# The first attention's scores for two tiles at a time, its last blocks of x in another order

## The chip, the cores and the metric

The kernel runs on one core of one Trainium2 chip. The metric is the device time of one execution in microseconds (us). Five engines work side by side, each through its own instructions in order: TensorE (PE, with its weight loads PEld), VectorE (DVE), ScalarE (ACT), GpSimd (POOL) and SyncE (SP), which here only issues DMAs. TensorE writes its results into PSUM, from where DVE and ACT read them.

## The reference, cut to what matters

Four batches of attention with 8 heads, 768 rows and 64 columns a head, a local window of 96 and 8 global columns; its output, as x with 512 columns, goes through a mixture of four experts of two matrix products each.

```python
scores = scale * np.matmul(q, k.transpose(0, 1, 3, 2)) + bias   # bias: -slope * distance
scores = np.where(keep, scores, -1e9)                           # local window or global column
a = np.exp(scores - scores.max(-1)); a = a / (a.sum(-1) + 1e-9)
x = np.matmul(a, v)                                             # as (3072, 512)
for e in range(4):
    h = np.maximum(x @ w1[e], 0.0)
    out += p[:, e:e + 1] * (h @ w2[e])
```

## The kernel before, in words

**Two stages that overlap.** Attention works on one batch, on four pairs of heads, on six tiles of 128 rows. The expert layers of a batch work on 16 units, each a quarter of an expert's hidden columns: `first(i)` makes h of unit i with seven products of 128x384 (a scheme that makes eight block products of four quarter blocks out of seven), `second(i)` multiplies h with w2 and adds into the output. Each product is six matmuls, since every operand is held as a high part and a rest. Attention of batch b+1 is spread between the products of batch b. Only the attention of batch 0 has nothing beside it: it is the **start** (lines 821 to 832), with pools of its own, and is meant in all that follows.

**The start's flow.** `attention` (line 482) yields once a tile, n = 0 to 23, and four times more to drain (n = 24 to 27). `flow` (line 488) is a software pipeline of four tiles: at step n it issues the scores of tile n, the biased maximum (DVE) and exponentials (ACT) of tile n-1, the normalisation (DVE) of tile n-2, the transposes of tile n-3 (`turn`: PE, then an ACT copy), and every third step `weigh`, the product with v for three tiles, copied by ACT into x. `scores` (line 382) writes the two heads of a tile into two tiles ps0 and ps1 of two buffers each. `AHEAD` (line 211) says after which tile the next quarter of the next pair's q and k is transposed and copied. The pairs come in the order 0, 2, 1, 3, so x[:, 3], the last to be ready, gets its first half at n = 24 and its second at n = 27.

**Blocks of x.** The seven products of `first` do not take x but sums of its quarters: B11, B21, B22 and T1 to T4, made by `blocks` (line 597): ACT copies the high part, DVE or POOL subtracts it to get the rest, and DVE forms the sums in place in x. `blocks(0, (0,), po)` makes the half that pairs 0 and 2 give, from n = 17 on; `blocks(0, (1,))` the half of pairs 1 and 3, after the loop (line 845).

**Weights.** `load_w1` and `load_w2` are generators. Each loads a raw tile by DMA, waits `lead` steps, and makes copies (ACT) and rests (POOL) of it; for w1, POOL also forms four sums first, then `hold` steps pass. `work_chores` (line 814) advances every chore in hand by one step at each yield. For batch 0 a finished w1s or w2s tile is also stored into DRAM (`keep`) for the other batches.

**Order.** While `Ordered.on` is set, each engine runs in program order: through the start and through `first(0)`. It is unset when `done` reaches `ONSTEPS` (line 868), the number of yields of `first(0)`; after that the planner may move instructions. At that point the loads of batch 1's q, k and v are issued too (`next(att)`).

**Products.** `product` (line 723) takes one of four PSUM buffers pm in turn, so a product cannot begin before the readers of the fourth before it are done. `relu` (line 748) lets ACT write h's high part and puts the rest into the list `late`; DVE does it at the next `add`, and it reads pm too.

Of the kernel before, what the change touches and what calls it, by code (L numbers as in the profile page):

```python
# [9 lines left out]
F32 = mybir.dt.float32  # L10
# [15 lines left out]
def f32(ap):  # L26
    return ap.bitcast(F32)
# [158 lines left out]
def attn_moe_kernel(ctx: ExitStack, tc, q, k, v, n_global, n_local, domain_probs, w1, w2, out):  # L186
# [21 lines left out]

    PAIRS = (0, 2, 1, 3)

    AHEAD = ((0, 1, 1, 1, 1, 1), (1, 1, 1, 1, 1, 0), (1, 1, 1, 1, 0, 0), (0,) * NQT)

    BIASES = ((0, 1), (0, 3), (1, 0), (1, 2))

    ONSTEPS = 7

    PL = P + NGLOB
    fast = main.enter_context(tc.tile_pool(name="fast", bufs=1))
# [160 lines left out]
        po.tensor_copy(vg[NPREV:], vt[:NGLOB, :, 0:1, :].to_broadcast([NGLOB, 2, NQT, D]))  # L379
        return vg  # L380

    def scores(A, t, got, early):


        if early:
            ps = [A.ps.tile([P, 512], F32, name=f"ps{j}") for j in range(2)]
        else:
            both = A.ps.tile([P, 2, 2 * P], F32, name="ps")
            ps = [both[:, j] for j in range(2)]
        c0 = max(t - 1, 0) * PL + (0 if t == 0 else NGLOB)  # L390
        n = P if t == 0 else 2 * P
        for j in range(2):
            if early:
                own = slice(j * D, (j + 1) * D)
                win = got["k"].rearrange("p t c -> p (t c)")[own, c0 : c0 + n]
                te.matmul(ps[j][:, :n], got["q"][own, t, :], win, start=True, stop=True)
                continue
            win = got["k"][:, j].rearrange("p t c -> p (t c)")[:, c0 : c0 + 2 * P]
            for part in range(2):
                te.matmul(  # L400
                    ps[j][:, : 2 * P],
                    got[("q", t // TPH)][:, j, part, t % TPH * P : (t % TPH + 1) * P],
                    win,
                    start=(part == 0),
                    stop=(part == 1),
                )
        return ps

    def softmax(A, new, old):

# [71 lines left out]
    def attention(b, A, early=False):  # L482


        x = xs[b] = xp.tile([P, NPAIR, S], F32, name="x")
        tiles, turned = [None] * 4, []

        def flow(new=None):

            one, two, three, four = tiles  # L490
            if new:
                new["ps"] = scores(A, new["t"], gots[new["pr"]], early)
            if four:
                turned.append(four)
            ready = len(turned) == TPH
            if ready and not early:
                weigh(A, turned, x)
            if three and not early:
                turn(A, three)
            softmax(A, one, two)  # L500
            if three and early:
                turn(A, three)
            if ready and early:
                weigh(A, turned, x)
            if ready:
                turned.clear()
            tiles[:] = [new, one, two, three]

        def start(pr):

            nats[pr] = {n: next(load(A, src, b, pr, n)) for n, src in (("q", q), ("k", k), ("v", v))}

        def prepare(nat, got):

            got["v"] = nat
            prepare_q(A, nat["q"], 0, got)
            yield 1
            prepare_k(A, nat["k"], 0, got)
            yield 1
            prepare_q(A, nat["q"], 1, got)  # L520
            yield 1
            prepare_k(A, nat["k"], 1, got)
            yield 1
            nat["vg"] = windows(A, nat["v"])
            yield 1
            yield 1

        def prepare_all(pr):
# [12 lines left out]
            yield 1  # L541

        nats, gots = {}, [{} for _ in range(NPAIR)]
        if early:
            halves = [load(A, src, b, 0, n, 2) for n, src in (("q", q), ("k", k))]
            bias = biases(start_stack.enter_context(tc.tile_pool(name="setup", bufs=1)))
            next(bias)
            nats[0] = dict(zip(("q", "k"), (next(h) for h in halves)))
            for h in halves:
                next(h)  # L550
            nats[0]["v"] = next(load(A, v, b, 0, "v"))
            todo = [prepare_all(pr) for pr in PAIRS]
            next(bias)
            next(todo[0])
            start(PAIRS[1])
        else:
            start(0)
            yield
        for m, pr in enumerate(PAIRS):
            cur = gots[pr]  # L560
            if not early:
                prep = prepare(nats[pr], cur)
                for _ in range(3):
                    next(prep)
                    flow()
                    yield
            for t in range(NQT):
                if early:
                    if t == 2 and m + 2 < NPAIR:
                        start(PAIRS[m + 2])  # L570
                elif t in (1, 2, 3):
                    next(prep)
                    flow()
                    yield
                if t == NQT - 1 and not early and m + 1 < NPAIR:
                    start(PAIRS[m + 1])
# [20 lines left out]
    def blocks(b, ks=(0, 1), low=ve):  # L597
# [38 lines left out]
        rest(low, "T4", b11)  # L636
        yield 1


    NPR = FF // (2 * P)  # L640
    units = [(b, e, g) for b in range(B) for e in range(E) for g in range(NPR)]
# [59 lines left out]
    def load_w2(i, lead=7):  # L701

        if i >= len(units):
            return
        b, e, g = units[i]
        if b > 0:
            wts[(i, 2)] = fetch("w2s", (e, g, 2), [P, 2, 2, DM], lambda t: t)
            return
        raw = rp.tile([P, 2, DM], F32, name="raw2")
        sy.dma_start(raw, w2[e, g * 2 * P : (g + 1) * 2 * P, :].rearrange("(a p) m -> p a m", p=P))  # L710
        for _ in range(lead):
            yield 1
        dst = wp.tile([P, 2, 2, DM], F32R, name="w2s")
        wts[(i, 2)] = dst
        for f in range(2):
            ac.copy(dst[:, 0, f], raw[:, f])
            po.tensor_tensor(dst[:, 1, f], raw[:, f], f32(dst[:, 0, f]), op=ALU.subtract)
            yield 1
        waiting[(i, 2)] = (e, g, 2), dst

    hs = {}

    def product(i, a, x):

        pm = ps_mm.tile([P, 512], F32, name="pm")
        m = 0
        for kt in range(2):
            for wi, xi in ((0, 0), (1, 0), (0, 1)):
                te.matmul(
                    pm[:, :HALF], wts[(i, 1)][a][:, wi, kt, :], xb[x][:, xi, kt, :], start=(m == 0), stop=(m == 5)  # L730
                )
                m += 1
        return pm
# [3 lines left out]
    def work_late():  # L737

        while late:
            lo, src, hi = late.pop()  # L740
            ve.scalar_tensor_tensor(lo, src, 0.0, f32(hi), op0=ALU.max, op1=ALU.subtract)

    def first(i):

# [14 lines left out]
            add(pm[:, :HALF], pm, other)  # L759
            return pm[:, :HALF]  # L760

        p1, u, vv = (up.tile([P, HALF], F32, name=n) for n in ("p1", "u", "vv"))
        keep(i, 1)
        pm = product(i, "A11", "B11")
        ac.copy(p1, pm[:, :HALF])
# [51 lines left out]
                chores.remove(c)  # L817

    bp = main.enter_context(tc.tile_pool(name="bp", bufs=1))
    Ordered.on = True  # L820
    with ExitStack() as start_stack:
        A = Pools(start_stack, "start", st=1, kd=2, qd=2, nat=2, natv=3, pb=4, ps=2, pt=3, px=1, early=True)
        for n, _ in enumerate(attention(0, A, early=True)):
            if n == 9:
                chores += [load_w1(0, lead=2), load_w2(0, lead=3)]
            if n == 18:
                chores.append(load_w1(1, lead=2, hold=3))
            if n == 2 * NQT + 5:
                chores.append(blocks(0, (0,), po))
            work_chores()  # L830
        mix = mixture()
        next(mix)
    Ordered.on = False
    hp = main.enter_context(tc.tile_pool(name="hp", bufs=2))
    up = main.enter_context(tc.tile_pool(name="up", bufs=1))
    op = main.enter_context(tc.tile_pool(name="op", bufs=1))
    ps_mm = main.enter_context(tc.tile_pool(name="ps_mm", bufs=4, space=PSUM))
    A = Pools(main, "att", st=1, kd=1, qd=1, nat=1, natv=1, pb=2, ps=2, pt=2, px=0, early=False)
# [3 lines left out]
    per = E * NPR  # L842
    count, span = NPAIR * (6 + NQT) + 5, (13 * per - 12) * 0.97
    Ordered.on = True
    chores.append(blocks(0, (1,)))
    for _ in range(2):
        work_chores()
    for b in range(B):
        att = attention(b + 1, A) if b + 1 < B else iter(())
        emitted = done = 0  # L850
# [67 lines left out]
```

## Time and profile before

| what | value |
|---|---|
| runs | 1203.73, 1201.08, 1203.69 us; median 1203.69 |
| the profiled execution, time | 1202.66 us |
| the profiled execution, span of the core | 1200.9 us |
| ACT busy over the span | 494.7 us (41%) |
| DVE busy over the span | 824.1 us (69%) |
| mean granted TensorE clock | 0.993 |

The span runs from the first instruction to the last. The profile also has an answer by stretches (busy time of every engine between two points of the span, with the granted clock of TensorE: 0.50 is half speed) and a timeline, whose rows are: start, duration, engine, line, operation, output<-inputs, shapes, count, and in brackets how long the engine had been idle before and what released it. All helpers' instructions carry line 42, so rows are told apart by the names of their tiles. "pt" are transposes, "ps" scores, "px" the products with v, "pm" the products of the expert layers, "xB" and "xT" the blocks of x, "raw" a weight tile as loaded.

### The profile page before, as it was taken

Reading aid. Unit: us, or ns where it says so; the run is one execution under the profiler, and the core shown is the slowest. Engines: PE = TensorE matmul, PEld = TensorE weight load, DVE = VectorE, ACT = ScalarE, POOL = GpSimd, SP = SyncE. Lnnn points to the kernel's source line nnn. Section 1 sums busy time; section 2 is a strip of 40 time slices with the busy share of each in tenths; the row PEclk is TensorE's granted clock in tenths of the full one; section 3 lists DMA queues with packets and bytes.
Section 4 is the critical chain, followed back from the end, with each engine's and each line's share of the span. In section 5 each row is a group of like instructions: output and inputs, shape, how many; then the busy total and the mean of one; then the engine's idle time right before and its main releaser. Section 6 shows DMA issues by size and latency. Waiting matters only on the chain.

```text
span 1200.9 us, 18119 instructions
## 1 busy us (share of the span) xinstructions
PE 1174.0 (98%) x6624; PEld 1045.0 (87%) x6624; DVE 824.1 (69%) x1858; ACT 494.7 (41%) x1268; POOL 210.7 (18%) x222
## 2 busy tenths in 40 slices
PE   7889999999999999999999999999999999999997
PEld 5677889989889989989888989989898999999996
DVE  7776567667678767676668767676666766666665
ACT  6865655565643444444342434444443211111110
POOL 4645655645440000000002000000000000000000
PEclk9899999999999999999999999999999999999999
DMA  7456777787878567565746757574663655544532
GB/s 169 119 198 214 259 288 245 288 292 234 325 253 265 191 198 239 187 220 176 240 169 205 248 186 228 196 231 163 219 206 132 245 194 193 187 178 181 190 132 90
DMA packets 122704, 251.39 MB, mean 209 GB/s; under 512 B 83184, under 2 KB 91376, under 8 KB 106224
## 3 DMA queue, kind: packets, MB, share of 16 engines
q1 hardware_dynamic: 118864, 243.87, 61.1%
q10 hardware_dynamic: 3744, 6.30, 1.4%
q8 instruction: 54, 0.88, 0.3%
q14 instruction: 42, 0.34, 0.1%
HBM read 174.11 MB, written 52.43 MB: 189 GB/s over the span
## 4 chain that ended last, share of the span: by engine, by line
PE 88%; DMA 3%; ACT 2%; issue 2%; POOL 2%; DVE 1%; SPq 1%; POOLq 0%; ACTq 0%; DVEq 0%
PE pm L42 77%; PE pt L42 7%; PE ps L42 4%; DMA raw<-in_moe_w_dram 2%; POOL sums L42 1%; PE px L42 1%; POOL w2s L42 1%; ACT pb L42 1%; SPq L42 1%; DMA qd<-st_q 1%; DMA q<-in_q_dram 0%; ACT xT L42 0%; DVE x L42 0%; ACT xB L42 0%; ACT h L42 0%
## 5 line engine op out<-in xcount | busy, mean ns | idle before, releaser
L42 PE MATMUL pm<-w2s,h 128*128 128x512 f32 x2304 | 551.7, 393 | 4.5 <-DVE h L42 4.5
L42 PEld LDWEIGHTS pm<-w2s,h 128*128 128x128 f32 x2304 | 426.1, 188 | 92.5 <-DVE h L42 6.3
L42 DVE SCALAR_TENSOR_TENSOR acc<-pm,prob,acc 128x512 f32<-128x512 f32 x360 | 268.2, 749 | 148.8 <-PE pm L42 146.5
L42 PE MATMUL pm<-xT,w1s 128*128 128x384 f32 x1536 | 296.7, 338 | 0.2 <-ACT xT L42 0.2
L42 PEld LDWEIGHTS pm<-xT,w1s 128*128 128x128 f32 x1536 | 267.8, 189 | 2.5 <-issue 1.4
L42 PE MATMUL pm<-xB,w1s 128*128 128x384 f32 x1152 | 226.8, 338 | 1.8 <-DVE xB L42 1.5
L42 PEld LDWEIGHTS pm<-xB,w1s 128*128 128x128 f32 x1152 | 201.3, 188 | 7.0 <-DVE xB L42 1.8
L42 ACT ACTIVATE h<-pm 128x384 fp32r<-128x384 f32 x256 | 124.8, 491 | 177.7 <-DVE pm L42 174.3
L42 DVE SCALAR_TENSOR_TENSOR h<-pm,h 128x384 fp32r<-128x384 f32 x256 | 140.9, 552 | 13.1 <-ACT h L42 9.5
L42 ACT ACTIVATE pb<-pb,nmax 128x256 f32<-128x256 f32 (+1 forms) x192 | 93.1, 487 | 95.3 <-DVE nmax L42 94.6
L42 ACT COPY p<-pm 128x384 f32<-128x384 f32 x64 | 30.7, 479 | 191.1 <-PE pm L42 182.0
L42 POOL COPY vg<-v 32x768 f32<-32x768 f32 x16 | 13.2, 828 | 498.6 <-DMA v<-in_v_dram 435.9
L42 DVE TENSOR_TENSOR u<-pm,p 128x384 f32<-128x384 f32 x64 | 35.6, 556 | 73.4 <-PE pm L42 53.5
L42 DVE CUSTOM_DVE_ANT_0 pb<-ps,nbias 128x256 f32<-128x256 f32 (+1 forms) x192 | 71.7, 397 | 10.5 <-PE ps L42 5.7
L42 ACT COPY pT<-pt 128x512 f32<-128x512 f32 (+1 forms) x96 | 52.6, 548 | 58.1 <-PE pt L42 57.8
L42 DVE TENSOR_TENSOR pm<-pm,vv 128x384 f32<-128x384 f32 x128 | 71.7, 560 | 1.6 <-PE pm L42 1.4
L42 ACT ACTIVATE pb<-pb,zsum 128x256 f32<-128x256 f32 (+1 forms) x144 | 63.3, 485 | 18.0 <-DVE zsum L42 18.0
L42 PE MATMUL pt<-ident,pb 128*128 128x128 f32 x352 | 58.3, 283 | 2.7 <-DVE pb L42 1.5
L42 PEld LDWEIGHTS pt<-ident,pb 128*128 128x128 f32 x352 | 42.2, 143 | 15.4 <-ACT pb L42 3.6
L42 DVE TENSOR_TENSOR vv<-pm,u 128x384 f32<-128x384 f32 x64 | 35.7, 557 | 27.1 <-PE pm L42 26.2
L42 DVE TENSOR_TENSOR u<-pm,u 128x384 f32<-128x384 f32 x64 | 35.7, 557 | 25.1 <-PE pm L42 24.4
L42 POOL TENSOR_TENSOR w2s<-raw,w2s 128x512 fp32r<-128x512 f32 x32 | 41.0, 1296 | 57.6 <-ACT w2s L42 57.6
(88 smaller groups left out, 887.3 us busy)
## 6 DMA issues: line engine op xcount, KB each, us to landing
w1s<-kept SPq DMA_DIRECT2D x48, 1792.0 KB, 7.4
w2s<-kept SPq DMA_DIRECT2D x48, 1024.0 KB, 4.9
kept<-w1s SPq DMA_DIRECT2D x16, 1792.0 KB, 9.5
qd<-st_q SPq DMA_DIRECT2D x96, 192.0 KB, 4.7
raw<-in_moe_w_dram SPq DMA_DIRECT2D x32, 512.0 KB, 5.6
kept<-w2s SPq DMA_DIRECT2D x16, 1024.0 KB, 6.7
v<-in_v_dram SPq DMA_DIRECT2D x16, 384.0 KB, 3.4
out_dram<-acc ACTq DMA_DIRECT2D x24, 256.0 KB, 3.9
```

The lines of the kernel that those rows point to most:

```text
L42: ins = fn(*args, **kwargs)
```

## The change

Scores of the first attention are made for two tiles at once: `scores_early` puts the two heads' scores of tiles t and t+1 into two halves of one ps tile each, at every even tile; at odd tiles nothing is issued. For that the second halves of the first pair's k and q come one step earlier (`AHEAD`). `blocks(0, (1,))` gives way to `last_blocks`, in six steps: B11 at n = 19, B21 at n = 26, B22 and T2 after the loop, then one step each for T1, T3 and T4 at the yields of `first(0)`. The first product, A11 with B11, moves into the drain of the attention (`opening`, n = 25), with a ps0 tile for a pm, and brings the store of the first w1s tile with it; the other six come in another order, and that of S4 with B22 keeps its buffer until vv is there. w2's first tile is made at n = 14 and 15 (`lead=5`) and not at 12 and 13; w1's second tile starts one step earlier, ahead of `blocks` in the list, with a `hold` of 2 for 3. `ONSTEPS` is 6, as `first(0)` now yields six times.

```diff
-    AHEAD = ((0, 1, 1, 1, 1, 1), (1, 1, 1, 1, 1, 0), (1, 1, 1, 1, 0, 0), (0,) * NQT)
+    AHEAD = ((1, 1, 0, 1, 1, 1), (1, 1, 1, 1, 1, 0), (1, 1, 1, 1, 0, 0), (0,) * NQT)
...
-    ONSTEPS = 7
+    ONSTEPS = 6
...
+    def scores_early(A, t0, got):
+        heads = [A.ps.tile([P, 2, 2 * P], F32, name=f"ps{j}") for j in range(2)]
+        for t in (t0, t0 + 1):
+            c0 = max(t - 1, 0) * PL + (0 if t == 0 else NGLOB)
+            n = P if t == 0 else 2 * P
+            for j in range(2):
+                own = slice(j * D, (j + 1) * D)
+                win = got["k"].rearrange("p t c -> p (t c)")[own, c0 : c0 + n]
+                te.matmul(heads[j][:, t - t0, :n], got["q"][own, t, :], win, start=True, stop=True)
+        return [[heads[j][:, i] for j in range(2)] for i in range(2)]
...
+                elif new["t"] % 2 == 0:
+                    new["ps"], ahead[0] = scores_early(A, new["t"], gots[new["pr"]])
+                else:
+                    new["ps"] = ahead[0]
...
+    def last_blocks():
+        b11, b12, b21, b22 = (
+            xs[0][:, k : k + 1, s] for k in (1, 3) for s in (slice(0, HALF), slice(HALF, S))
+        )
...
+        high("B11", b11)
+        rest(po, "B11", b11)
+        yield 1
+        high("B21", b21)
+        rest(ve, "B21", b21)
+        yield 1
+        high("B22", b22)
+        ve.tensor_sub(b12, b22, b12)
+        ve.tensor_add(b11, b12, b11)
+        rest(ve, "B22", b22)
+        high("T2", b11)
+        rest(ve, "T2", b11)
+        yield 1
+        ve.tensor_sub(b22, b22, b11)
+        high("T1", b22)
+        rest(ve, "T1", b22)
+        yield 1
+        high("T3", b12)
+        rest(po, "T3", b12)
+        yield 1
+        ve.tensor_sub(b11, b21, b11)
+        high("T4", b11)
+        rest(ve, "T4", b11)
+        yield 1
...
+    def opening(A):
+        ups.append(sums_of_products())
+        keep(0, 1)
+        pm = product(0, "A11", "B11", A.ps.tile([P, 512], F32, name="ps0"))
+        ac.copy(ups[0][0], pm[:, :HALF])
...
+        if i == 0:
+            p1, u, vv = ups.pop()
+            relu(0, 0, last(product(i, "A12", "B21"), p1))
+            yield
+            pm4 = product(i, "S4", "B22")
+            yield
+            add(u, product(i, "S2", "T2"), p1)
+            yield
+            add(vv, product(i, "S1", "T1"), u)
+            relu(0, 1, last(pm4, vv))
+            yield
+            pm = product(i, "S3", "T3")
+            add(u, pm, u)
+            relu(1, 1, last(pm, vv))
+            yield
+            relu(1, 0, last(product(i, "A22", "T4"), u))
+            yield
+            return
...
             if n == 9:
-                chores += [load_w1(0, lead=2), load_w2(0, lead=3)]
-            if n == 18:
-                chores.append(load_w1(1, lead=2, hold=3))
+                chores += [load_w1(0, lead=2), load_w2(0, lead=5)]
             if n == 2 * NQT + 5:
-                chores.append(blocks(0, (0,), po))
+                chores += [load_w1(1, lead=2, hold=2), blocks(0, (0,), po)]
             work_chores()
+            if n == 3 * NQT + 1:
+                last = last_blocks()
+                next(last)
+            if n == 4 * NQT + 1:
+                opening(A)
+            if n == 4 * NQT + 2:
+                next(last)
...
-    chores.append(blocks(0, (1,)))
-    for _ in range(2):
-        work_chores()
+    chores.append(last)
+    work_chores()
```

More of the change, by code (lines that the diff above doesn't have):

```diff
@@ L380, in windows, with scores @@
         return vg
[L382 to L389, printed above, removed]
+    def scores(A, t, got):
+        both = A.ps.tile([P, 2, 2 * P], F32, name="ps")
         c0 = max(t - 1, 0) * PL + (0 if t == 0 else NGLOB)
-        n = P if t == 0 else 2 * P
         for j in range(2):
[L393 to L397, printed above, removed]
             win = got["k"][:, j].rearrange("p t c -> p (t c)")[:, c0 : c0 + 2 * P]
@@ L400, in scores @@
                 te.matmul(
-                    ps[j][:, : 2 * P],
+                    both[:, j],
                     got[("q", t // TPH)][:, j, part, t % TPH * P : (t % TPH + 1) * P],
@@ L406, in scores @@
                 )
-        return ps
+        return [both[:, j] for j in range(2)]
+    def scores_early(A, t0, got):
[8 more added lines that the diff above has]
+        return [[heads[j][:, i] for j in range(2)] for i in range(2)]
     def softmax(A, new, old):
@@ L485, in attention @@
         x = xs[b] = xp.tile([P, NPAIR, S], F32, name="x")
-        tiles, turned = [None] * 4, []
+        tiles, turned, ahead = [None] * 4, [], [None]
         def flow(new=None):
@@ L491, in flow @@
             if new:
-                new["ps"] = scores(A, new["t"], gots[new["pr"]], early)
+                if not early:
+                    new["ps"] = scores(A, new["t"], gots[new["pr"]])
+                elif new["t"] % 2 == 0:
+                    new["ps"], ahead[0] = scores_early(A, new["t"], gots[new["pr"]])
+                else:
+                    new["ps"] = ahead[0]
             if four:
@@ L637, in blocks, with high, rest @@
         yield 1
+    def last_blocks():
+        b11, b12, b21, b22 = (
+            xs[0][:, k : k + 1, s] for k in (1, 3) for s in (slice(0, HALF), slice(HALF, S))
+        )
+        def high(name, src):
+            ac.copy(xb[name][:, 0, 1:2], src)
+        def rest(eng, name, src):
+            eng.tensor_tensor(xb[name][:, 1, 1:2], src, f32(xb[name][:, 0, 1:2]), op=ALU.subtract)
+        high("B11", b11)
[22 more added lines that the diff above has]
+        yield 1
     NPR = FF // (2 * P)
@@ L721, in attn_moe_kernel, with product @@
     hs = {}
-    def product(i, a, x):
-        pm = ps_mm.tile([P, 512], F32, name="pm")
+    def product(i, a, x, pm=None):
+        if pm is None:
+            pm = ps_mm.tile([P, 512], F32, name="pm")
         m = 0
@@ L741, in work_late, with sums_of_products @@
             ve.scalar_tensor_tensor(lo, src, 0.0, f32(hi), op0=ALU.max, op1=ALU.subtract)
+    ups = []
+    def sums_of_products():
+        return [up.tile([P, HALF], F32, name=n) for n in ("p1", "u", "vv")]
+    def opening(A):
[3 more added lines that the diff above has]
+        ac.copy(ups[0][0], pm[:, :HALF])
     def first(i):
@@ L760, in last @@
             return pm[:, :HALF]
-        p1, u, vv = (up.tile([P, HALF], F32, name=n) for n in ("p1", "u", "vv"))
+        if i == 0:
[16 more added lines that the diff above has]
+            return
+        p1, u, vv = sums_of_products()
         keep(i, 1)
@@ L819, in attn_moe_kernel @@
     bp = main.enter_context(tc.tile_pool(name="bp", bufs=1))
+    up = main.enter_context(tc.tile_pool(name="up", bufs=1))
     Ordered.on = True
@@ L834, in attn_moe_kernel @@
     hp = main.enter_context(tc.tile_pool(name="hp", bufs=2))
-    up = main.enter_context(tc.tile_pool(name="up", bufs=1))
     op = main.enter_context(tc.tile_pool(name="op", bufs=1))
```

## The prediction, made before the changed kernel was run

> **What bounds the kernel now.** I read the page first: the shares and the chain that ended last.
>
> ```profile
> PE 1174.0 (98%) x6624; PEld 1045.0 (87%) x6624; DVE 824.1 (69%) x1858; ACT 494.7 (41%) x1268; POOL 210.7 (18%) x222
> ...
> PE 88%; DMA 3%; ACT 2%; issue 2%; POOL 2%; DVE 1%; SPq 1%; POOLq 0%; ACTq 0%; DVEq 0%
> ```
>
> TensorE sets the time nearly everywhere, and the change takes no matmul away. What it can win lies where PE waits or runs slowly: the start, up to about 81 us. Elsewhere it can win nothing; it can only move what the planner does after `first(0)`. So I read the start by stretches, cut where the granted clock (third number from the end) changes.
>
> ```profile
> core 0: us, PE busy (x) PEld busy (x) DVE busy (x) ACT busy (x) POOL busy (x), PEclk, DMA share, GB/s
> 22.00:35.00 13.00, 13.00 (x119) 8.86 (x116) 11.37 (x72) 12.48 (x40) 3.71 (x5) 1.00 0.69 186
> 36.40:39.80 3.40, 1.45 (x11) 1.00 (x11) 1.20 (x10) 2.67 (x9) 3.32 (x5) 0.98 0.01 3
> 39.80:43.00 3.20, 3.20 (x24) 2.23 (x24) 1.87 (x13) 3.20 (x12) 3.10 (x4) 0.50 0.01 3
> 49.90:53.30 3.40, 2.34 (x13) 1.17 (x10) 2.53 (x15) 2.57 (x11) 2.18 (x3) 1.00 0.38 18
> 53.30:60.10 6.80, 6.80 (x39) 4.75 (x38) 6.68 (x37) 4.73 (x16) 5.45 (x7) 0.50 0.01 4
> 63.50:66.90 3.40, 2.48 (x28) 1.88 (x28) 2.54 (x16) 3.40 (x11) 1.64 (x2) 1.00 0.01 2
> 70.40:73.90 3.50, 1.94 (x8) 1.33 (x9) 2.89 (x5) 0.89 (x2) 0.92 (x1) 0.99 0.94 393
> 73.90:77.20 3.30, 3.30 (x12) 3.10 (x11) 2.34 (x5) 1.34 (x3) 1.97 (x2) 0.50 1.02 417
> ```
>
> In 22 to 35 PE and ACT are both full (13.00 and 12.48 of 13.0). Then come three holes in PE (1.45 of 3.4, 2.34 of 3.4, 1.94 of 3.5), and behind each the clock is 0.50, for 3.2, 6.8 and 3.3 us. A stretch with 2.48 of 3.4 stayed at 1.00. So here a window of 3.4 us that is a third empty costs half speed in the next.
>
> **The change, part by part. w2 later.**
>
> ```profile
> 36.01 0.73 POOL L42 TENSOR_TENSOR sums<-raw 128x256 f32<-128x256 f32 x1 [6.91 <-DMA raw<-in_moe_w_dram]
> ...
> 37.13 0.62 ACT L42 CAST w2s<-raw 128x512 fp32r<-128x512 f32 x1 [2.24 <-DMA raw<-in_moe_w_dram]
> ...
> 43.55 0.82 POOL L42 COPY vg<-v 32x768 f32<-32x768 f32 x1 [0.65 <-POOL w2s L42]
> ...
> 47.20 1.28 POOL L42 TENSOR_TENSOR w1s<-sums,w1s 128x512 fp32r<-128x512 f32 x1 [0.70 <-ACT w1s L42]
> 49.50 1.97 POOL L42 TENSOR_TENSOR xB<-x,xB 128x384 fp32r<-128x384 f32 x2 [1.01 <-ACT xB L42]
> ...
> 51.49 0.56 DVE L42 TENSOR_TENSOR x<-x 128x384 f32<-128x384 f32 x1 [0.83 <-POOL xB L42]
> ```
>
> ACT, in order, stands 2.24 us at n = 12 for the raw w2, with the exponentials of the next tile behind it; hence the hole at 36.4. Two steps later the tile is long there, and w1's raw tile, which the copy at n = 13 needs, was there at 36.01. The two copies themselves only move. **What is late next is POOL**: it starts with w1's landing, and its rests must be done before those of the blocks at 49.50, which DVE awaits. From 36.01 to 48.48 POOL stood idle 0.65 and 0.70 us, both behind ACT; without these it ends at 47.13, the blocks' two rests at 49.1, and DVE's sum starts 2.4 us earlier than at 51.49. So the gain is ACT's, **-2.25**; it is 1.0 if POOL keeps its gaps (49.50 would then move by its wait of 1.01 alone).
>
> **Scores for two tiles.** The work of PE, DVE and ACT is the same. Saved is one change between scores and transposes per pair.
>
> ```profile
> 7.39 1.66 PE L42 MATMUL ps<-early_k,early_q 64*128 64x128 f32 x8 [0.57 <-ACT early_k L42]
> 8.97 0.90 PE L42 MATMUL pt<-ident,k 128*128 128x128 f32 x3
> ...
> 15.01 1.23 PE L42 MATMUL ps<-early_k,early_q 64*128 64x256 f32 x4
> 16.17 1.11 PE L42 MATMUL pt<-ident,pb 128*128 128x128 f32 x4
> ...
> 59.56 0.48 ACT L42 COPY x<-px 128x384 f32<-128x384 f32 x1 [1.79 <-PE px L42]
> ```
>
> One tile alone takes 16.17 - 15.01 = 1.16 us before the clock is up, the narrow first and the second tile together 1.58. I put the saving at 0.2 to 0.3 us for a pair, some 2 us of PE in all, but ACT, 96% busy in 22 to 35, lets only 0.5 of 13 through. Against it: in the first steps k's second half now stands ahead of the first exponentials on ACT, and a pair of scores (2.3 us at half speed) ahead of `turn`, for which ACT then waits. I count the first 20 us at 0 (from -1.0 to +0.7) and the rest at **-0.3**. PE's waits for a free ps buffer go as well, but the hole at 49.9 has DVE and POOL behind it: in n = 17 to 20 PE has no transposes of q and k left, so I let the half-speed stretch of 53 to 60 stand; if it goes, ACT's wait of 1.79 goes too.
>
> **Weights and blocks ahead of the end.** w1's second tile is copied at n = 21 to 24 and not 23 to 26, so two more copies stand ahead of the last exponentials, on an ACT that is full there (3.40 of 3.40 in 63.5 to 66.9).
>
> ```profile
> 66.03 0.42 ACT L42 CAST w1s<-raw 128x256 fp32r<-128x256 f32 x1
> ...
> 66.82 0.64 ACT L42 CAST w1s<-sums 128x512 fp32r<-128x512 f32 x1
> ...
> 68.73 0.48 ACT L42 COPY x<-px 128x384 f32<-128x384 f32 x1 [0.28 <-PE px L42]
> ```
>
> That is 0.42 + 0.64: **+1.0**. B11's copy at n = 19 (some 0.5, like the copy of x) falls ahead of ACT's wait of 1.79 and is hidden there; without that wait it costs its 0.5. The copies of p1 and of B21 take the places in the drain that two of the weights' copies leave: 0. POOL gets B11's rest on top, in a stretch where it is not the last. `opening`'s six matmuls fall into PE's empty 0.9 of the stretch 63.5 to 66.9: 0, at most +0.2.
>
> **The end: blocks and products.** All instants from here on are counted from the last copy into x, 68.73.
>
> ```profile
> 68.62 0.79 PE L42 MATMUL pm<-xB,w1s 128*128 128x384 f32 x3
> ...
> 79.55 1.30 PE L42 MATMUL pm<-xT,w1s 128*128 128x384 f32 x6
> 80.69 1.21 PE L42 MATMUL pm<-xB,w1s 128*128 128x384 f32 x6
> ...
> 69.25 1.22 DVE L42 TENSOR_TENSOR x<-x 128x384 f32<-128x384 f32 x1 [2.62 <-ACT x L42]
> ...
> 73.38 0.55 DVE L42 TENSOR_TENSOR x<-x 128x384 f32<-128x384 f32 x1
> ...
> 74.52 0.55 DVE L42 TENSOR_TENSOR xT<-x,xT 128x384 fp32r<-128x384 f32 x1
> ...
> 85.05 0.56 DVE L42 TENSOR_TENSOR u<-pm,u 128x384 f32<-128x384 f32 x1
> ...
> 88.65 0.55 DVE L42 SCALAR_TENSOR_TENSOR h<-pm,h 128x384 fp32r<-128x384 f32 x1
> ```
>
> Before, the last product begins at 79.55, or 10.8, and ends at 12.0. After, PE has its matmuls early: A12 with B21 needs nothing new. But there are four buffers pm, and the sixth product, A22 with T4, takes that of S4 with B22, which is held until vv is added, ACT has made h of it and DVE the rest, and that rest is emitted only behind the sum of the **fifth** product. In DVE's order these are 15 instructions: four for B12, B11, B22 and T2, the sum of A12, two for T1, u and a rest of h, two for T4, vv, the sum of S4, u, the rest of h. Eight such in a row take (88.65 - 85.05) / 7 = 0.51 each. So 15 take 7.7; T1 and T4 each wait for ACT between the sum and the rest (74.52 - 73.38 = 1.14, against 0.51, twice 0.63); DVE begins at 0.5 (69.25), and T2's wait and POOL's rest of T3 beside it (an instruction beside POOL took 1.22 at 69.25) add 0.3. The sixth product begins at 9.7 and, with 80.69 - 79.55 = 1.1, ends at 10.8: **-1.2**. PE has done the fifth at about 7.0 (it waits for the ninth DVE instruction, 5.9, for its own buffer) and stands still from 7.0 to 9.7. A window of 3.4 us that is four fifths empty is emptier than any of the three that were followed by clock 0.50; the dense products behind it then run at half speed for at least 3.3 us, which costs half of that, and part of a second window by where it falls: 1.65 to 3.4, I take **+1.9**. What the end of `blocks` before lost by its own stretch at 0.50 (73.90 to 77.20) is within its 12.0.
>
> Sum: -2.25 - 0.3 + 1.0 - 1.2 + 1.9 = **-0.85**. On the profiled execution's 1202.66 us (span 1200.9 and 1.8 around it) this gives **1201.8**. That execution is 1.0 below the median of the runs, 1203.69, and between their ends, so I do not correct for it.
>
> **The rivals. Gate open.** The wait at the end doesn't reach half speed, by the windows' phase or because DVE is quicker: 1201.8 - 1.9 = 1199.9; if the stretch at 53 to 60 goes as well (PE has two tiles' scores to go on with while DVE waits), 1199.9 - 1.8 = 1198.1. Against it stand the three holes, the mildest of which (2.34 of 3.4) was enough. The Trainium skill, "TensorE: Matmul & The Clock Gate", section "Why this matters for your kernels", asks for no idle gap over about 3 us; by that rule the 2.7 us would be let through and the sum be the first of these two times. The trace disagrees with it: the hole at 70.4 to 73.9 has no gap of 3 us in it and cost the clock.
>
> **Given back to POOL.** w2's gain stays at 1.0 for 2.25: 1201.8 + 1.25 = 1203.0. For it speaks that POOL is 3.32 of 3.40 busy in 36.4 to 39.8, against it that both its gaps end with ACT.
>
> **Slower: SP's queue.** `first(0)` now has six yields, and the seventh step of `load_w1(2, 6, 3)`, its DMA, comes only after batch 1's q, k and v are issued.
>
> ```profile
> 73.32 5.79 SPq L42 DMA_DIRECT2D q<-in_q_dram  x2
> ...
> 84.83 0.99 SPq L42 DMA_DIRECT2D v<-in_v_dram  x1
> ...
> 89.70 1.43 POOL L42 TENSOR_TENSOR sums<-raw 128x256 f32<-128x256 f32 x2
> ...
> 94.42 2.51 POOL L42 TENSOR_TENSOR w1s<-sums,w1s 128x512 fp32r<-128x512 f32 x2
> ...
> 99.29 0.68 PE L42 MATMUL pm<-xB,w1s 128*128 128x384 f32 x3
> ...
> raw<-in_moe_w_dram SPq DMA_DIRECT2D x32, 512.0 KB, 5.6
> ```
>
> If SP keeps that order, the tile lands at 85.8 + 5.6 = 91.4 at best, where POOL used it at 89.70; POOL ends at 96.9 and PE wants it at 99.29, so it costs nothing until the landing passes 92.1, and each us beyond is paid. Loads that crowd each other as q's did (5.79 us for two issues) could add 5: 1201.8 + 5 = 1206.8. Against it: behind `first(0)` the planner may put a load whose buffer is free earlier.
>
> **How the numbers follow.** Chances: the forecast 0.45, open gate 0.27, given back 0.16, SP's queue 0.12. What a measurement of this kernel can tell from no change is about 0.3%, 3.6 us: faster is below 1200.1, slower above 1207.3. Faster: three quarters of the open gate (0.20) and a fifth of the forecast's own spread of 2 us (0.09): 0.29. Slower: under half of SP's queue (0.05) and 0.03 for the planner's order behind it: 0.08. Within: 0.63. The range reaches from a little below the open gate's second time, 1197.5, to SP's case, 1206.0.
>
> **What would show it.** ACT's copy of w2 without a wait, and POOL's two rests of xB ended 2 us earlier. Pairs of ps as x8. The last copy into x at 68.73 - 1.5 = 67.2 (it takes the first three terms). Behind it six products of pm, the sixth 2.7 us after the fifth with a release by DVE h, and clock 0.50 after it. The forecast is wrong at its root if the sixth product follows at once, if ACT still waits 2 us for a DMA, or if PE waits for w1s near 100 us.

## The result and the profile after

The changed kernel takes 1190.66 us (median of four runs, 1190.10 to 1190.96); the kernel before, on the same chip, 1202.51. The ratio is 0.9904, with an interval of 0.9888 to 0.9921. The prediction was 1201.8 with a range of 1197.5 to 1206.0: the time lies below the range, and the gain is 11.85 us where 0.85 was forecast. One execution of all that follow, 1934.47 us of the kernel without the pairs, is far slower than the rest and is left out of its numbers.

The profiled execution took 1190.1 us, its span 1188.3, which is 12.6 us under the span before. First the page of the changed kernel, its shares and its chain:

```profile
PE 1164.0 (98%) x6624; PEld 1039.9 (88%) x6624; DVE 825.5 (69%) x1859; ACT 493.9 (42%) x1268; POOL 210.8 (18%) x221
...
PE 92%; ACT 3%; DVE 2%; DMA 1%; issue 1%; POOL 0%; SPq 0%; DVEq 0%; POOLq 0%
```

PE has the same 6624 instructions, 10 us less of busy time, and 92% of the chain for 88%. DMA went from 3% of the chain to 1%, POOL from 2% to 0%: a first hint that waits for weights are gone. Where the 12.6 us went is read from three landmarks, each of which is one row in either timeline. Timeline of the kernel before, the first product with v, and then the same landmark, the last copy into x and the products around the end of `first(0)` in the kernel after (start, duration, engine, operation, in brackets the wait):

```profile
21.01 0.44 PE L42 MATMUL px<-pT,v 128*64 128x128 f32 x4
```

```profile
18.35 0.44 PE L42 MATMUL px<-pT,v 128*64 128x128 f32 x4
...
63.31 0.48 ACT L42 COPY x<-px 128x384 f32<-128x384 f32 x1 [0.35 <-PE px L42]
...
63.20 2.20 PE L42 MATMUL pm<-xB,w1s 128*128 128x384 f32 x11
66.87 0.44 PE L42 MATMUL pm<-xB,w1s 128*128 128x384 f32 x1 [1.47 <-DVE xB L42]
67.15 5.24 PE L42 MATMUL pm<-xT,w1s 128*128 128x384 f32 x24
72.41 1.34 PE L42 MATMUL pm<-xB,w1s 128*128 128x384 f32 x6
...
74.12 0.62 PE L42 MATMUL pm<-xT,w1s 128*128 128x384 f32 x2 [0.38 <-DVE h L42]
```

| stretch | before | after | gain | predicted |
|---|---|---|---|---|
| to the first product with v | 21.01 | 18.35 | 2.7 | 0 |
| from there to the last copy into x | 47.7 | 45.0 | 2.8 | 1.55 |
| from there to the first product of unit 1 (80.69, 72.41) | 12.0 | 9.1 | 2.9 | 1.2, less 1.9 for the clock |
| from there to the end of the span | 1120.2 | 1115.9 | 4.3 | 0 |

Every stretch gave more than was forecast, and the largest item lies where the prediction says "elsewhere it can win nothing". There the windows tell of it. Each row begins with the window and its length; PE's busy time comes next, and the clock is the third number from the end; the kernel before, then the kernel after:

```profile
80.00:100.00 20.00, 18.19 (x97) 16.17 (x96) 15.20 (x34) 7.33 (x16) 10.55 (x11) 1.00 0.58 153
100.00:120.00 20.00, 18.91 (x101) 16.67 (x101) 13.65 (x35) 12.71 (x35) 10.11 (x11) 1.00 0.83 281
120.00:140.00 20.00, 18.18 (x112) 16.02 (x111) 11.39 (x28) 12.20 (x33) 10.50 (x11) 1.00 1.02 351
140.00:160.00 20.00, 20.00 (x128) 18.12 (x128) 13.39 (x31) 10.30 (x27) 8.66 (x10) 1.00 0.66 216
160.00:180.00 20.00, 18.02 (x95) 16.27 (x95) 11.87 (x25) 12.25 (x32) 15.02 (x17) 1.00 0.70 254
```

```profile
80.00:100.00 20.00, 18.59 (x98) 16.37 (x97) 16.61 (x37) 9.92 (x25) 9.78 (x10) 1.00 0.66 217
100.00:120.00 20.00, 20.00 (x107) 17.98 (x106) 14.16 (x34) 11.05 (x29) 9.83 (x10) 1.00 0.82 295
...
sum 100.00, PE 98.59 PEld 88.25 DVE 71.67 ACT 58.37 POOL 57.45; mean PE 19.72 PEld 17.65 DVE 14.33 ACT 11.67 POOL 11.49
```

In these 100 us PE stood idle 6.7 us before (18.19 + 18.91 + 18.18 + 20.00 + 18.02 = 93.3) and stands 1.4 after. Who held it is said by the chain of the same stretch (80 to 200 us), before and after:

```profile
by line: PE pm L42 30.7%; DMA raw<-in_moe_w_dram 18.2%; issue 14.2%; POOL sums L42 8.9%; POOL w2s L42 7.0%; SPq L42 4.2%; PE pt L42 2.0%; ACT pb L42 1.7%; PE ps L42 1.6%; ACT w2s L42 1.6%; ACT w1s L42 1.6%; ACT h L42 1.2%; POOL w1s L42 1.0%
```

```profile
by line: PE pm L42 83.6%; PE pt L42 8.6%; PE ps L42 4.7%; DVE kd L42 1.1%; DVE pm L42 0.9%; DVE u L42 0.5%; DVE h L42 0.4%; DVE vv L42 0.4%; issue 0.1%
```

Before, the chain ran through the preparation of weights: a raw tile's DMA, POOL's rests of w2s, POOL's sums of w1, ACT's copy of the sums. After, none of these is on it. One turn of it, in the timeline of the kernel before:

```profile
119.67 2.55 POOL L42 TENSOR_TENSOR w2s<-raw,w2s 128x512 fp32r<-128x512 f32 x2 [5.55 <-ACT w2s L42]
122.16 1.44 POOL L42 TENSOR_TENSOR sums<-raw 128x256 f32<-128x256 f32 x2
...
124.33 0.62 ACT L42 CAST w1s<-sums 128x512 fp32r<-128x512 f32 x1 [2.49 <-POOL sums L42]
...
126.28 0.62 ACT L42 CAST w1s<-sums 128x512 fp32r<-128x512 f32 x1 [1.23 <-POOL sums L42]
126.81 0.90 ACT L42 ACTIVATE pb<-pb,zsum 128x256 f32<-128x256 f32 x2
127.62 0.84 ACT L42 ACTIVATE h<-pm 128x384 fp32r<-128x384 f32 x2
...
128.12 0.56 DVE L42 SCALAR_TENSOR_TENSOR h<-pm,h 128x384 fp32r<-128x384 f32 x1 [1.46 <-ACT h L42]
...
128.73 3.06 PE L42 MATMUL pm<-w2s,h 128*128 128x512 f32 x12 [1.82 <-DVE h L42]
```

Read it from the bottom: PE waits 1.82 for DVE's rest of h, DVE 1.46 for ACT's ReLU, and ACT, in order, had stood 2.49 and 1.23 for POOL's sums with that ReLU queued behind. POOL came to the sums only at 122.16 because w2's two rests stood ahead of them and had waited 5.55 for ACT's own copy of w2. So ACT waits for POOL, which had waited for ACT. I call this the **detour**. The experiments ask whether it is the cause.

The obvious rival is that the raw tile of w1 simply lands late; the DMAs have the second largest share of the chain. In the turn shown it is not so: that tile was issued at 111.63 and landed 5.4 us later, at 117.0, while POOL stood idle until 119.67. In the turn before, it is: the tile was issued at 98.6, took 6.9 us, and the sums began as it landed, at 105.60. So both occur in this stage.

### The profile page after: what moved, and what is told of

Its sections match the earlier page's. It is cut to its first block, busy times and chain, and to the rows that moved or that the text cites. A ratio compares the mean times of both kernels' runs of the same rounds, so it can differ in the third digit from the quotient of the medians.

```text
span 1188.3 us, 18090 instructions
## 1 busy us (share of the span) xinstructions
PE 1164.0 (98%) x6624; PEld 1039.9 (88%) x6624; DVE 825.5 (69%) x1859; ACT 493.9 (42%) x1268; POOL 210.8 (18%) x221
## 4 chain that ended last, share of the span: by engine, by line
PE 92%; ACT 3%; DVE 2%; DMA 1%; issue 1%; POOL 0%; SPq 0%; DVEq 0%; POOLq 0%
PE pm L42 82%; PE pt L42 7%; PE ps L42 3%; ACT pb L42 1%; DVE pb L42 1%; DMA qd<-st_q 1%; DVE x L42 0%; DMA q<-in_q_dram 0%; ACT xT L42 0%; ACT pT L42 0%; ACT w1s L42 0%; PE px L42 0%; POOL w1s L42 0%; ACT xB L42 0%; ACT x L42 0%
## 5 line engine op out<-in xcount | busy, mean ns | idle before, releaser
L42 DVE SCALAR_TENSOR_TENSOR h<-pm,h 128x384 fp32r<-128x384 f32 x256 | 140.4, 551 | 10.8 <-ACT h L42 7.6
```

The costliest lines, as they stand in the source:

```text
L42: ins = fn(*args, **kwargs)
```

## The experiments

**One part alone, and all parts but one.** The change falls into four parts that can be applied singly: pairs of scores with the new `AHEAD`; w2 later; w1's second tile earlier; and the tail (`last_blocks`, `opening`, the order of the products, `ONSTEPS` 6). The diffs, in that order:

```diff
-    AHEAD = ((0, 1, 1, 1, 1, 1), (1, 1, 1, 1, 1, 0), ...
+    AHEAD = ((1, 1, 0, 1, 1, 1), (1, 1, 1, 1, 1, 0), ...
+    def scores_early(A, t0, got):
...
-                chores += [load_w1(0, lead=2), load_w2(0, lead=3)]
+                chores += [load_w1(0, lead=2), load_w2(0, lead=5)]
...
-            if n == 18:
-                chores.append(load_w1(1, lead=2, hold=3))
-                chores.append(blocks(0, (0,), po))
+                chores += [load_w1(1, lead=2, hold=2), blocks(0, (0,), po)]
...
+    def last_blocks():
+    def opening(A):
-    ONSTEPS = 7
+    ONSTEPS = 6
```

Pairs alone:

> The kernel before with the scores for two tiles and the new AHEAD alone. Clock theory: PE stands dense from 9 us on, TensorE reaches full speed near 12 us and not at 19, the first product with v begins near 18.4 and not at 21.0, and the whole run is 2 to 4 us shorter. Rival (fewer changes between scores and transposes, clock unchanged): full speed still comes at 19 us, the gain is below 1 us.

w2 alone:

> The kernel before with w2's first tile two steps later alone. If the prediction's term holds: ACT's wait of 2.24 us for the load is gone and the last copy into x is 2 us earlier, the run some 2 us shorter. Rival: the wait passes on to POOL or to the loads and less than 1 us is left.

w1 alone:

> The kernel before with w1's second tile one step earlier and a hold of 2 alone. Prediction's term: two more copies ahead of the last exponentials, +1.0 us. Queue theory (behind the start, loads of the next weights stand on SP behind the store of w1's second tile, which waits for POOL): that store is ready earlier, so the loads go out some 2 to 5 us earlier and waits of PE behind 90 us get shorter: -1 to -3 us.

The tail alone:

> The kernel before with the blocks, the first product in the drain and the new order of products alone (with ONSTEPS 6). Queue theory: the planner puts the load of w1's third tile ahead of the store of the second, PE's waits near 95, 111, 129 and 170 us go, and with the shorter end (9.1 us from the last copy into x to the end of the first unit's products, not 12.0) the run is 6 to 8 us shorter. Rival (what lies behind 72 us came only from all being earlier): 2.7 us shorter, the waits remain.

All but the pairs:

> The changed kernel with single scores and the old AHEAD again. Clock theory: full speed at 19 us again, the first product with v near 21, and 3 to 5 us of the 12 are lost. Rival (clock unchanged by it): under 1 us is lost.

All but w2:

> The changed kernel with w2's first tile at the old place. If the term of the prediction holds here too, ACT waits some 2 us for the load again and 2 us are lost. Rival: with the start running earlier the loads come at another moment and nothing is lost.

All but w1:

> The changed kernel with w1's second tile at the old place and hold 3. Prediction's term: 1 us faster than the changed kernel. Queue theory: the store of w1's second tile and the load of the third go out later; 1 to 2 us slower.

All but the tail:

> The changed kernel with the old end: blocks after the loop, all seven products in the old order, ONSTEPS 7. Queue theory: SP has the loads of the next weights behind the store of w1's second tile again, PE waits behind 90 us, 5 to 8 us are lost. Rival: only the 2.7 us of the end itself are lost and no waits come back behind 90 us.

| kernel | us | ratio to before, interval | last copy into x | PE idle behind 80 us |
|---|---|---|---|---|
| before | 1202.51 | 1 | 68.73 | 7.7 |
| pairs alone | 1198.93 | 0.9973 (0.9961 to 0.9984) | 64.10 | 7.7 |
| w2 alone | 1196.47 | 0.9954 (0.9926 to 0.9981) | 62.04 | 9.2 |
| w1 alone | 1204.27 | 1.0013 (1.0000 to 1.0026) | 69.44 | 9.4 |
| tail alone | 1196.80 | 0.9959 (0.9943 to 0.9976) | 67.92 | 5.1 |
| all but pairs | 1192.83 | 0.9927 (0.9901 to 0.9952) | 65.91 | 2.6 |
| all but w2 | 1193.26 | 0.9927 (0.9907 to 0.9947) | 66.28 | 2.4 |
| all but w1 | 1192.73 | 0.9920 (0.9900 to 0.9939) | 62.03 | 5.1 |
| all but tail | 1203.12 | 1.0005 (0.9992 to 1.0018) | 64.32 | 10.1 |
| changed kernel | 1190.66 | 0.9904 (0.9888 to 0.9921) | 63.31 | 3.0 |

(The last column sums the windows from 80 to 1180 us. Each ratio is to the kernel before as it ran beside that kernel: 1201.66 us for the parts alone, 1201.89 for all but one, 1202.51 for the changed kernel.)

Against the expectations: pairs alone gained the 2.7 us that the clock theory asked for, though the clock column reads 1.00 all through the first 20 us and can't show its mechanism. All but w2 lost 2.6 for an expected 2, and all but w1 lost 2.1, near what the queue theory had (1 to 2), where the prediction's term had a gain of 1. The others missed: w2 alone gained 5.2 for 2; w1 alone lost 2.6, where the prediction's term had 1.0 and the queue theory a gain; the tail alone gained 4.9 for 6 to 8; all but the pairs lost 2.2 for 3 to 5; all but the tail lost 12.5 for 5 to 8.

Three things follow. The parts don't add up: three of them together give nothing without the tail, although the start is 4.4 us shorter. What takes it back is the last column, 10.1 us of idle PE, and in that kernel a stretch at half speed behind 243 us besides. And most of the tail's worth is not at the end of `blocks`, which without the tail is only 1.6 us longer: it is in the last column too. This is the detour in the kernel without the tail, in its timeline, and then a wait there that has another cause:

```profile
97.58 1.30 POOL L42 TENSOR_TENSOR w2s<-raw,w2s 128x512 fp32r<-128x512 f32 x1 [8.30 <-ACT w2s L42]
98.84 1.44 POOL L42 TENSOR_TENSOR sums<-raw 128x256 f32<-128x256 f32 x2
...
101.00 0.62 ACT L42 CAST w1s<-sums 128x512 fp32r<-128x512 f32 x1 [2.10 <-POOL sums L42]
102.92 0.62 ACT L42 CAST w1s<-sums 128x512 fp32r<-128x512 f32 x1 [1.30 <-POOL sums L42]
103.56 0.87 ACT L42 ACTIVATE h<-pm 128x384 fp32r<-128x384 f32 x2
...
104.70 1.66 PE L42 MATMUL pm<-w2s,h 128*128 128x512 f32 x6 [3.18 <-DVE h L42]
...
241.51 0.62 ACT L42 CAST w1s<-raw 128x512 fp32r<-128x512 f32 x1 [4.25 <-DMA raw<-in_moe_w_dram]
...
242.51 0.49 ACT L42 ACTIVATE h<-pm 128x384 fp32r<-128x384 f32 x1
243.04 0.56 DVE L42 SCALAR_TENSOR_TENSOR h<-pm,h 128x384 fp32r<-128x384 f32 x1 [4.84 <-ACT h L42]
```

At 241.51 ACT, with h's ReLU queued behind, waits for the raw tile itself; PE's wait of 2.8 us for h and the stretch at half speed follow. Here the load is late and POOL's order has no part in it.

**Which line of the tail? `ONSTEPS` alone.** With 6 the planner may move instructions one product earlier, and the next raw tile of w1 goes ahead of the two stores on SP. The number alone was changed in the kernel before, in the kernel without the tail, and back to 7 in the changed one:

```diff
-    ONSTEPS = 7
+    ONSTEPS = 6
```

> The kernel before with ONSTEPS 6 for 7 and nothing else: the planner may move instructions one product earlier. The computation is the whole one. Theory A (order): the waits behind 80 us come from the order in which weights are prepared. With 6, the raw tile of w1(2) is issued on SP ahead of the two kept stores, and POOL forms its four sums ahead of w2's rests, so ACT finds the sums ready and h's relus do not queue behind it. Then the start stays as before (last copy into x at 68 to 69.5), PE's waits behind 95 us fall from about 8 us (1.81, 1.09, 1.82, 2.0 and smaller) to under 4, and the time is 1197 to 1199.5. Theory B (phase: the waits shift with the start's length and have nothing to do with ONSTEPS): 1200.5 to 1203, waits of the same sum, at other places.

> The kernel without the last part (blocks and products in the old order) but with ONSTEPS 6: it differs from the one that took 1203.1 in that constant alone. The computation is the whole one. Theory A (order): PE's waits behind 80 us go, and the start that is 4.4 us shorter comes through: 1194 to 1198. Theory B (the new blocks and products themselves are needed): 1201.5 to 1204.

> The changed kernel with ONSTEPS 7: the planner is set free only after the first product of first(1). The raw tile of w1(2) then stands on SP behind the store of w1(1) and the load of w2(1), and w2's rests stand on POOL ahead of the sums of w1(2), as before the change. The computation is the whole one. Theory A (order): the start up to 72.4 us stays, PE waits behind 80 us come back in part, 1193.5 to 1197. Theory B: 1189.5 to 1192.5, no wait of PE over 1 us behind 85 us.

Measured were 1200.28 (ratio 0.9993, 0.9980 to 1.0006), 1191.52 (0.9919, 0.9892 to 0.9946) and 1188.53 (0.9890, 0.9864 to 0.9916). One number is worth 11.6 us in the kernel without the tail (1203.12 to 1191.52), and the new blocks and products are not needed for it. But theory A, that the earlier load always cures, missed twice: in the kernel before nothing that can be measured is gained, and in the changed kernel 7 is not worse but 2 us better. So the tail cures the stage in either of two ways: by `ONSTEPS` 6 with the old products, or by its new blocks and products with `ONSTEPS` 7. The number is a switch between orders, not the cause. In the kernel before, PE's idle time behind 80 us fell to 4.9 us only, and PE keeps two waits of 1.34 and 1.88 us (for the exponentials at 108 us and for h at 167 us).

What 7 improves in the changed kernel is seen in its start. The changed kernel first, then the one with 7 (timelines of DVE, POOL and PE):

```profile
62.65 1.74 POOL L42 TENSOR_TENSOR sums<-raw 128x256 f32<-128x256 f32 x2
...
63.83 1.98 DVE L42 TENSOR_TENSOR x<-x 128x384 f32<-128x384 f32 x2
65.73 1.08 DVE L42 TENSOR_TENSOR xB<-x,xB 128x384 fp32r<-128x384 f32 x1
```

```profile
65.09 1.22 DVE L42 TENSOR_TENSOR x<-x 128x384 f32<-128x384 f32 x2 [0.27 <-ACT x L42]
66.23 0.55 DVE L42 TENSOR_TENSOR xB<-x,xB 128x384 fp32r<-128x384 f32 x1
...
66.84 0.45 PE L42 MATMUL pm<-xB,w1s 128*128 128x384 f32 x1 [0.19 <-DVE xB L42]
...
70.39 3.22 POOL L42 TENSOR_TENSOR w2s<-raw,w2s 128x512 fp32r<-128x512 f32 x2
73.58 1.41 POOL L42 TENSOR_TENSOR sums<-raw 128x256 f32<-128x256 f32 x2
```

With 6, POOL's sums for unit 2 run beside two of DVE's sums of x and the rest of B22, and these three take 3.06 us where they take 1.77 without POOL beside them; PE's wait for xB is 1.47 against 0.19. With 7 the sums come at 73.58, behind w2's rests, and still in time, because w2's rests did not have to wait there: ACT then waits only 0.7 us for sums in 72 to 140 us. So not every rest ahead of a sum makes a detour, only one that has to wait for ACT.

**Take the detour away with one number.** In the stage behind the start, w1's load, sums and copies begin after seven steps and not after nine, so that POOL reaches the sums ahead of w2's rests. The load moves with them, so the edit also helps where the tile lands late; it does not separate the two.

```diff
-                chores.append(load_w1(i + 2, 9) if fn is first else load_w2(i + 2))
+                chores.append(load_w1(i + 2, 7) if fn is first else load_w2(i + 2))
```

> The kernel before, with the preparation of w1 (load, sums, copies) begun at the seventh step of a product stage and not the ninth, for every unit behind the start. The computation is the whole one and the start is untouched. Theory C (detour): PE's waits behind 80 us come from POOL's order. Where a rest of w2s, which waits for ACT's copy, stands ahead of the four sums of w1 (before: 87.19, 104.34, 119.67), ACT waits in its turn for those sums, with h's ReLU queued behind it, then DVE's rest of h, then PE. Two steps earlier the sums stand ahead of the rests on POOL. Then ACT's waits at the copies of sums in 72 to 140 us fall from 8.7 to under 4, PE's idle time behind 80 us falls from 7.7 to under 4, and the time is 1197 to 1199.5. Theory B (phase: waits of about the same sum at other places whenever the order changes): 1200.5 to 1204.

> The kernel without the last part (blocks and products in the old order), with the same edit of one number. The computation is the whole one. Theory C: PE's idle time behind 80 us, 10.1 before the edit with the waits of 3.2, 1.5 and 2.8 for h, falls to under 4 and the half speed behind the last goes with it; the start's gain comes through: 1193 to 1197, from 1203.1. Theory B: 1200.5 to 1204.

> The changed kernel with the same edit. The computation is the whole one. It has POOL's sums ahead of w2's rests nearly everywhere already, and only 3.0 us of idle time of PE behind 80 us, of which 1.4 stand at 82 to 84 us (a wait for kd and one for h) that this edit does not touch. Theory C: 1189.5 to 1191.5. Theory B: anywhere from 1189 to 1196.

> The changed kernel with ONSTEPS 7, which took 1188.5 and has 1.3 us of idle time of PE behind 80 us, with the same edit. The computation is the whole one. Theory C: nothing is left to take away, 1187.5 to 1189.5. Theory B: 1188 to 1195.

| kernel with this edit | without | with | ratio to before, interval | PE idle behind 80 us |
|---|---|---|---|---|
| before | 1201.32 | 1195.35 | 0.9944 (0.9922 to 0.9965) | 7.7 to 3.6 |
| all but tail | 1203.12 | 1191.57 | 0.9912 (0.9893 to 0.9932) | 10.1 to 2.7 |
| changed kernel | 1190.66 | 1191.25 | 0.9912 (0.9887 to 0.9937) | 3.0 to 2.4 |
| changed, `ONSTEPS` 7 | 1188.53 | 1187.98 | 0.9888 (0.9862 to 0.9914) | 1.3 to 1.3 |

Theory C has the right sign in all four: 6 and 11.5 us where the detour was, nothing measurable where it wasn't. The first two gained more than its ranges (1195.35 for 1197 to 1199.5, 1191.57 for 1193 to 1197). In the kernel before, PE's idle time fell by 4.1 us, less than the 6.0; in all but the tail, the wait behind the late load at 241.51 is gone along with the detour. The fastest versions are the last two, some 2 us under the changed kernel: the runs don't overlap (1187.34 to 1188.75 for `ONSTEPS` 7 alone, 1190.10 to 1190.96 for the changed kernel), though the intervals of the ratios do. The kernel before with this edit also shows a control within one trace (timeline):

```profile
85.58 2.55 POOL L42 TENSOR_TENSOR w2s<-raw,w2s 128x512 fp32r<-128x512 f32 x2 [9.80 <-ACT w2s L42]
88.10 1.43 POOL L42 TENSOR_TENSOR sums<-raw 128x256 f32<-128x256 f32 x2
...
93.85 0.55 PE L42 MATMUL pt<-ident,q 128*128 128x128 f32 x3 [1.81 <-DVE st_q L42]
...
101.86 1.43 POOL L42 TENSOR_TENSOR sums<-raw 128x256 f32<-128x256 f32 x2 [5.66 <-DMA raw<-in_moe_w_dram]
...
106.60 2.55 POOL L42 TENSOR_TENSOR w2s<-raw,w2s 128x512 fp32r<-128x512 f32 x2
```

w1's tile of unit 2 comes from another line, which the edit leaves: there w2's rests stay ahead of the sums (85.58, 88.10), and PE's wait of 1.81 stays to the hundredth (at 95.45 before). From unit 3 on the sums go first (101.86, 106.60), and the waits at 110.70, 128.73 and 170.18 are gone. One point of the expectation missed: ACT's waits at the copies of sums in 72 to 140 us fell from 8.7 to 6.2 us and not under 4. Two waits of 1.3 us are left at 133 and 135 us which PE doesn't feel. So the sum of ACT's waits is not the measure; what counts is what is queued behind each.

**The slow first 18 us.** Sixteen transposes of the identity, whose result nobody reads, were put ahead of q's first transposes in the changed kernel:

```diff
+        idle = A.ps.tile([P, 512], F32, name="ps0")
+        for _ in range(16):
+            te.transpose(idle[:, :P], ident, ident)
```

> The changed kernel with 16 transposes of the identity into an unused ps0 tile ahead of the first transposes of q, which begin at 5.3 us: work whose result nobody reads. The computation is the whole one. If TensorE is slow in the first 18 us because it has not been busy (three transposes of 128 columns took 0.87 us at 5.3), they take under 0.5 us there now, the first product with v comes at 16 to 17.5 us and not 18.35, and the time is 1188 to 1190. If the loads of q, k and v bound these 18 us (DMA share 1.1 to 1.25 until 18 us), 1190 to 1191.5.

The time is 1190.94 (ratio 0.9910, 0.9884 to 0.9935): no change. Timeline of PE:

```profile
1.34 3.68 PE L42 MATMUL ps<-ident 128*128 128x128 f32 x16 [1.34 <-POOL ident masks.py:199]
5.29 0.52 PE L42 MATMUL pt<-ident,q 128*128 128x128 f32 x3 [0.27 <-DMA q<-in_q_dram]
```

The three transposes that took 0.87 take 0.52 (under 0.5 was expected), so PE had been slow and is hardly so any longer, and yet the first product with v comes at 18.13 for 18.35, and not at 16 to 17.5. In these 18 us PE's speed is not the limit; that the loads are was the rival, and it fits, but it wasn't tried by itself.

## Why the prediction was wrong

**"Elsewhere it can win nothing" is the step that failed.** The prediction took a PE that is 98% busy for a stage that can't be improved, and cut its windows only up to 77 us. Behind 80 us 7.7 us of PE's idle time stood in the trace of before, in a few waits of 1 to 2 us, and the share of POOL and DMA in its chain showed them. It did name the lever, though as a danger: that the planner moves a load and POOL's sums with it. The rival of **SP's queue** had the sign wrong: the tile of w1 was issued at 57.30, well ahead of batch 1's q, k and v, and not behind them; before the change, SP issued w2's and w1's tiles from 70.94 on. (The range's upper end, 1206.0, is called SP's case, which the prediction itself puts at 1206.8.) What the stage had to give is measured best by the edit of one number in the kernel before: 6.0 us (4.2 to 9.4 by the interval), for the detour and for loads that come late. It came with the change because the tail set another order, not because the forecast had a term for it.

**The start.** Forecast was 1.55 us up to the last copy into x, and the two profiles show 5.4. Part of that is the executions: three kernels with the old start (before, with 6, with the edit of one number) have this copy at 68.73, 66.49 and 67.29, and five with the new one at 63.31 to 65.19, with 64.44 in the middle. By the middle ones it is 2.9 us. With the edit of one number on both sides, pairs, w2 and w1 together are worth 3.8 us (1195.35 to 1191.57). By terms:

- **w2 later, 2.25:** right in its mechanism. ACT's copy has no wait (35.76), POOL's rests of the blocks end 5.6 us earlier, at 45.83, of which 2.7 us are the earlier first product with v. The rival that POOL keeps the gain is out. In the whole kernel the term measures 2.6 us (1193.26 without it); why it is worth 5.2 alone stays open. One reading was wrong: POOL's 0.65 us at 43.55 ended with POOL's own w2s, not with ACT.
- **Pairs in the first 20 us, 0:** mis-sized. Without pairs six profiles have the first product with v at 19.64 to 21.01 and one at 18.07; with pairs ten have it at 18.35 to 18.76. The middle ones (19.96 and 18.67) differ by 1.3 us, and the spread is gone. How the pairs save it is not shown.
- **w1 earlier, a loss of 1.0:** the runs agree, though within the spread of the executions: the last copy into x comes 1.3 us earlier without it (62.03 for 63.31), and w1 alone gives 1.0013. In the whole kernel it costs nothing, since all but w1 is 2.1 us slower, with 2.1 us more idle PE behind 80 us.

**The end, a gain of 1.2 and a loss of 1.9.** Both fell with one premise, that the four buffers pm are taken in turn. The last products follow each other at once (67.15, x24 without a gap), which is the very sign that the prediction named as its refutation. The sixth product, A22 with T4, begins near 71.0, while DVE reads the buffer of S4 with B22 only at 72.39; so it took another, that had come free before. So it ends at 9.1 behind the last copy and not at 10.8, and the idle window that was to cost the clock doesn't exist. At the same full clock the old order takes 10.7 (64.32 to 75.03 without the tail), so the new one saves 1.6, near the 1.2 for another reason. But these 1.6 us are not in the time: with the edit of one number, all but the tail takes 1191.57 and the changed kernel 1191.25. In the latter PE waits 0.65 and 0.71 us for kd and h behind the first products of unit 1, against 0.89 for h without the tail; that accounts for 0.5 of the 1.6, and the rest stays open. With `ONSTEPS` 7 these waits are gone, and the changed kernel's wait for xB of 1.47 us as well.

**The clock.** The rule "a third empty costs half speed in the next" is wrong. Windows of the kernel after:

```profile
36.40:42.40 6.00, 4.01 (x28) 2.51 (x28) 3.92 (x23) 6.00 (x21) 5.59 (x6) 0.99 0.44 137
42.40:45.70 3.30, 3.30 (x26) 2.64 (x25) 2.60 (x12) 3.26 (x11) 2.29 (x3) 0.50 1.14 457
...
46.00:60.10 14.10, 9.45 (x85) 6.53 (x85) 12.55 (x72) 12.52 (x40) 11.09 (x12) 1.00 0.49 138
```

In 36.4 to 42.4 a third is empty, and 3.3 us at 0.50 follow; in 46.0 to 60.1 a third is empty as well, with gaps of 1.05, 1.66 and 1.34 us, and the clock stays at 1.00. Cut finer, 38.9 to 42.3 has PE busy 2.05 of 3.4 and half speed behind it, 49.1 to 52.5 has 1.82 and full speed. Three cases of the trace before were too few for a rule.

In the profile after, the stretches at 0.50 between 53 and 60 and behind 74 are gone: 10.1 us at half speed, which can have cost at most 5.0 us. Both were parts of the rival of the open gate, but only one of them holds. In all five profiles with the new start the clock of 60 to 80 us is 1.00 (0.91, 0.74 and 0.83 with the old), while in 40 to 60 us it is 0.91, 0.91, 0.83, 0.83 and 0.83: from one execution to the next, about 3.5 or 7 us at half speed are left there. The Trainium skill, "TensorE: Matmul & The Clock Gate", section "What's actually happening", has a free-running activity window of about 3.4 us. The stretch of 3.3 us agrees. That it matters where in such a window a gap falls would be one explanation, but no run here shows it: the two windows just compared lie three such lengths apart, and the emptier one cost nothing. What decides stays open.

Added up along this one path, each to a microsecond or two: 6.0 us for the stage behind the start, 3.8 for the start and 0.3 for the tail make 10.1. Measured were 11.85 against four runs of the kernel before; against the 11 to 24 runs of it in the experiments (1201.32 to 1201.89) the same 1190.66 is a gain of 10.7 to 11.2.

## What to carry to other kernels

When PE is 98% busy, 2% of 1200 us is still 24 us: list its waits over the whole span and read the chain of that stretch, before saying that a stage can't give anything. An engine in order that prepares data for a later step (ACT's copy of a sum here) passes its wait on to whatever urgent work is queued behind it, so look for loops in which two engines wait for each other in turn, and cure them by starting the later of the two preparations earlier; that was one number. And before an edit's gain in one stage is credited, test it with the stage behind it settled: the same three edits of the start were worth nothing with the detour (1201.89 to 1203.12) and 3.8 us without it (1195.35 to 1191.57).

## What was not expected of the hardware

- Two of DVE's sums of x, with both inputs in SBUF, took 1.98 us beside POOL's sums and 1.22 without; a rest took 1.08 and 0.55. The Trainium skill, "GPSIMD Engine Reference", section "Specifications", has POOL's access to SBUF shared with VectorE and contention for DVE instructions with two SBUF inputs; the rows agree.
- The page's granted clock is 1.00 in the first 18 us, and yet three transposes take 0.87 us there and 0.52 after 3.7 us of transposes before them. So here a PE that had had no work was slow without the clock column showing it.
- The first product with v came at 18.07 to 21.01 us in kernels with the same instructions up to there, so a difference of up to 3 us between two single profiles of this start need not come from an edit.
